# The first two half sequences of sliding-window attention: new loads, V and keys placed by products, distances added by TensorE

## The chip, the core and the metric

One core of one Trainium2 chip runs the kernel. The metric is its device time in microseconds (us), lower is better. One launch computes all four sequences and the feed-forward layer behind them.

## What is computed

The attention has four sequences of 768 tokens, 8 heads of 64. A query sees the 96 tokens up to itself and 8 global tokens at the sequence's start; the score falls with the distance, by a slope for each head. A gated layer follows (3072 tokens, 512 to 1536 to 512).

```python
scores = scale * np.matmul(q, k.transpose(0, 1, 3, 2))
rel = pos[:, None] - pos[None, :]
is_global = pos[None, :] < int(n_global)
is_local = (rel >= 0) & (rel < int(n_local))
keep = is_global | is_local
dist = np.where(is_global & ~is_local, float(n_local), np.abs(rel).astype(np.float32))
scores = scores - slopes[:, None, None] * dist[None, :, :]
scores = np.where(keep, scores, -1000000000.0)
a = np.exp(scores - np.max(scores, axis=-1, keepdims=True))
a = a / (np.sum(a, axis=-1, keepdims=True) + 1e-09)
x = np.matmul(a, v)   # then (tokens, heads * 64)
out = (np.maximum(x @ w_gate, 0.0) * (x @ w_val)) @ w_out
```

## The kernel before, in words

The work is cut into eight **halves** `s`: half `s % 2` of sequence `s // 2`, 384 queries each. In a half the heads go by **pairs** `p` (0 to 3). Queries lie on partitions as rows of three tokens (`(p n)`, n = 3), so a loaded row of q or k holds 768 bytes a head. The keys of a sequence lie in seven **key tiles** `j` of 128: the 8 global keys in rows 0 to 7, then 120 keys in order. A half meets tiles 0 to 3, or 2 to 6, each over a window of at most 72 x 3 queries (`spans`, `by`, `banks_of_half`). Of tile 3, half 0 has only 24 keys; columns 32 to 127 of `kT[..][p][:, 3]` are zeroed first, since a score product takes all 128 columns as its weights.

Every engine runs its instructions in the order in which the program writes them (`manual_schedule`). GpSimd (POOL) issues the loads that convert fp32 to bf16 (V and the weights), SyncE (SP) the others, q and k in fp32.

The first two halves of the kernel before:

- **Loads** (L110): q and k of half 0 by pairs on SP. V comes by key tile on POOL (`load_v`, L129, up to 120 rows x 8 heads of 64 numbers, 960 pieces), the global rows of V apart (L120) and spread to the other tiles by SP (L125). Weights in three groups for gate and value (L146, 512 pieces each).
- **Setup**: POOL makes the distances `dd` (L177 to L189), VectorE those of the global rows (L194 to L201). ScalarE turns them into the multiplicative masks `m_all`, eight exponentials of 432 columns (L209), and zeroes the unused halves of q (L203, L204). VectorE zeroes the unused columns of key tile 3 (L467, L470).
- **A pair**: `piece_cast` (L223) casts q and k by VectorE in half 0, by GpSimd in half 1. `piece_t` (L254) transposes them on TensorE, and VectorE copies q into two zero-padded halves (L259, L260) and k to key tiles (L238 to L244). `piece_qk` multiplies a key tile with both heads' queries at once (L306); ScalarE takes the exponential (L309), VectorE multiplies the mask (L318). `piece_av_wide` makes the sums (weights `ones`) and the values (weights V) of both heads in column halves of the array (L366), ScalarE takes lnd = ln and rcp = exp(-lnd) of the sums (L372, L374), and VectorE multiplies the values with rcp into `xT` (L377).
- The pairs of half 1 are woven with the first gate and value products of half 0's tokens (`ffn_pieces`: gate L408, relu L411, value L418, multiply L420, output L427). The first gate product of half 1's tokens needs `xT` of all four pairs of half 1; the products that follow it form a full queue on TensorE to the end.

PSUM has 8 banks: three for scores and transposes (`qk_ps`), two for `av_ps`, three for `ff_ps`. Halves 2 to 7 take another way (casts on GpSimd, transposes by DMA) that the change leaves as it is, except for where `m_all` is made.

## Time and profile before

| | |
|---|---|
| time, median of 3 runs | 258.38 us (258.17 to 259.35) |
| profiled execution, span from first to last instruction | 256.7 us (the page gives no other time of it) |
| busy TensorE | 236.1 us, 92% |
| busy ScalarE, VectorE, GpSimd | 159.0, 140.9, 93.6 us |
| granted TensorE clock | 1.000 |
| last multiply of half 0 into xT, start and duration (L377) | 24.74, 0.56 us |
| the same of half 1 | 41.64, 0.56 us |
| HBM read, mean | 135 GB/s over the span |

The profile lists each instruction's start and duration, and for idle time what ended it. Durations of TensorE products include a tail in which the next one already runs: four products of 384 columns, 326 ns each, take 0.65 us together. Several equal instructions are merged into one line with a count ("x4").

### The profile page before, as it was taken

Reading aid. Unit: us, or ns where it says so; the run is one execution under the profiler, and the core shown is the slowest. Engines: PE = TensorE matmul, PEld = TensorE weight load, DVE = VectorE, ACT = ScalarE, POOL = GpSimd, SP = SyncE. Lnnn points to the kernel's source line nnn. Section 1 sums busy time; section 2 is a strip of 40 time slices with the busy share of each in tenths; the row PEclk is TensorE's granted clock in tenths of the full one; section 3 lists DMA queues with packets and bytes.
Section 4 is the critical chain, followed back from the end, with each engine's and each line's share of the span. In section 5 each row is a group of like instructions: output and inputs, shape, how many; then the busy total and the mean of one; then the engine's idle time right before and its main releaser. Section 6 shows DMA issues by size and latency. Waiting matters only on the chain.

```text
span 256.7 us, 4693 instructions
## 1 busy us (share of the span) xinstructions
PE 236.1 (92%) x1608; PEld 138.7 (54%) x1608; DVE 140.9 (55%) x369; ACT 159.0 (62%) x321; POOL 93.6 (36%) x232
## 2 busy tenths in 40 slices
PE   1467888999999999999999999999999999999994
PEld 0235554566554566655665566556665566556541
DVE  6785895564644276625674376725763557614410
ACT  8747485333578577756875577747774677643311
POOL 8951796057635605800645145500640000000000
PEclk9999999999999999999999999999999999999999
DMA  6999699997967993856571975927451200021012
GB/s 167 204 190 234 167 195 200 231 153 153 278 83 191 189 299 70 142 79 190 171 147 11 195 250 114 116 82 223 129 125 42 82 3 0 0 82 43 0 41 83
DMA packets 82696, 34.35 MB, mean 134 GB/s; under 512 B 58609, under 2 KB 79601, under 8 KB 82673
## 3 DMA queue, kind: packets, MB, share of 16 engines
q1 hardware_dynamic: 50816, 26.16, 38.0%
q0 software_dynamic: 31856, 7.91, 31.3%
q8 instruction: 12, 0.20, 0.4%
q14 instruction: 12, 0.09, 0.1%
HBM read 28.38 MB, written 6.29 MB: 135 GB/s over the span
## 4 chain that ended last, share of the span: by engine, by line
PE 77%; DVE 11%; DMA 5%; ACT 3%; issue 1%; SPq 1%; POOL 0%; DVEq 0%; ACTq 0%; POOLq 0%
PE ff_ps L427 24%; PE ff_ps L418 22%; PE ff_ps L408 21%; PE av_ps L334 5%; PE qk_ps L306 4%; DMA ks<-in_k_dram 4%; DVE xT L351 2%; DVE es L318 2%; DVE ht L420 2%; PE qk_ps L254 1%; DVE qk L223 1%; DMA qs<-in_q_dram 1%; ACT lnd L343 1%; ACT rcp L348 1%; DVE qT L260 1%
## 5 line engine op out<-in xcount | busy, mean ns | idle before, releaser
L408 PE MATMUL ff_ps<-xT,wg 128*128 128x384 bf16 x384 | 78.4, 326 | 0.6 <-DVE ks L158 0.4
L418 PE MATMUL ff_ps<-xT,wv 128*128 128x384 bf16 x384 | 78.0, 326 | 0.6 <-DVE ht L420 0.3
L411 ACT ACTIVATE grelu<-ff_ps 128x384 bf16<-128x384 f32 x96 | 47.0, 489 | 38.3 <-DVE ht L420 21.9
L420 DVE TENSOR_TENSOR ht<-ff_ps,grelu 128x384 bf16<-128x384 f32 x96 | 53.2, 555 | 27.5 <-PE ff_ps L418 23.9
L427 PE MATMUL ff_ps<-wo_sb,ht 128*128 128x512 bf16 x288 | 67.1, 379 | 0.0
L309 ACT ACTIVATE es<-qk_ps 128x432 bf16<-128x432 f32 (+2 forms) x96 | 49.4, 529 | 17.9 <-PE qk_ps L306 15.5
L318 DVE TENSOR_TENSOR es<-es,m_all 128x432 bf16<-128x432 bf16 (+6 forms) x144 | 43.0, 335 | 22.9 <-ACT es L309 22.4
L351 DVE TENSOR_TENSOR xT<-av_ps,rcp 64x384 bf16<-64x384 f32 x48 | 26.7, 555 | 45.7 <-ACT rcp L348 41.2
L418 PEld LDWEIGHTS <-wv 128*128 128x128 bf16 x384 | 36.4, 97 | 24.2 <-issue 2.8
L408 PEld LDWEIGHTS <-wg 128*128 128x128 bf16 x384 | 36.3, 98 | 22.9
L427 PEld LDWEIGHTS <-ht 128*128 128x128 bf16 x288 | 26.9, 97 | 27.8
L306 PE MATMUL qk_ps<-qT,kT 128*128 128x432 bf16 (+6 forms) x144 | 33.7, 303 | 1.6 <-ACT es L309 1.2
L264 POOL CAST kc<-ks 128x384 bf16<-128x384 f32 x24 | 12.3, 552 | 55.8 <-DMA ks<-in_k_dram 47.9
L343 ACT ACTIVATE lnd<-av_ps 64x384 f32<-64x384 f32 x48 | 23.3, 485 | 11.1 <-PE av_ps L334 10.4
L432 ACT COPY osb<-ff_ps 128x512 f32<-128x512 f32 x24 | 14.0, 585 | 24.4 <-PE ff_ps L427 23.5
L129 POOL DMA_DIRECT2D vbuf<-in_v_dram x28 | 24.4, 879 | 0.8 <-issue 0.4
L334 PEld LDWEIGHTS <-vbuf 128*128 128x128 bf16 x216 | 18.1, 98 | 8.2 <-issue 0.7
L334 PE MATMUL av_ps<-es,vbuf 128*128 128x216 bf16 (+4 forms) x216 | 21.1, 226 | 0.5 <-DVE xT L351 0.5
L306 PEld LDWEIGHTS <-kT 128*128 128x128 bf16 x144 | 14.3, 102 | 12.2 <-issue 3.1
L272 POOL CAST qz<-qs 128x192 bf16<-128x192 f32 x48 | 14.8, 356 | 3.6 <-DMA qs<-in_q_dram 3.6
L254 PE MATMUL qk_ps<-ident,qk 128*128 128x128 bf16 x48 | 5.3, 265 | 11.6 <-DVE qk L223 9.1
L348 ACT ACTIVATE rcp<-lnd 128x384 f32<-128x384 f32 x24 | 12.5, 522 | 0.8
(68 smaller groups left out, 111.6 us busy)
## 6 DMA issues: line engine op xcount, KB each, us to landing
out_dram<-osb SPq DMA_DIRECT2D x24, 256.0 KB
ks<-in_k_dram SPq DMA_DIRECT2D x6, 768.0 KB
qs<-in_q_dram SPq DMA_DIRECT2D x6, 768.0 KB
vbuf<-in_v_dram POOLq DMA_DIRECT2D x24, 120.0 KB, 5.8
ks<-in_k_dram SPq DMA_DIRECT2D x8, 192.0 KB
qs<-in_q_dram SPq DMA_DIRECT2D x8, 192.0 KB
wg<-in_moe_w_gate_dram POOLq DMA_DIRECT2D x3, 512.0 KB, 7.4
wv<-in_moe_w_val_dram POOLq DMA_DIRECT2D x3, 512.0 KB, 9.2
```

Of the source, the lines that this page charges most:

```text
L129: nc.gpsimd.dma_start(out=v_dst(b, NG + r0, NG + r0 + n, j), in_=v[b, :, KT * j + r0 : KT * j + r0 + n, :].rearrange("h p d -> p h d"))
L306: nc.tensor.matmul(ps[:, c : c + n_], lhsT=kt[:, j, :], rhs=qd[:, :, :, a : a + w], start=True, stop=True)
L309: nc.scalar.activation(es[:, 0:cols], ps[:, 0:cols], AF.Exp, bias=0.0, scale=scale)
L318: nc.vector.tensor_mul(e4, e4, mk)
L334: nc.tensor.matmul(av3[:, :, a : a + w], lhsT=vb[:, j, z0 : z0 + 128], rhs=es[:, c : c + NN * w].rearrange("k (n p) -> k n p", n=NN), star ...
L343: nc.scalar.activation(ln[o0 : o0 + 64], av[d0 : d0 + 64, 0:QH], AF.Ln, bias=0.0, scale=1.0)
L351: nc.vector.tensor_tensor(xT_of[s][r, p, :], av_of[s, p, e_][r, 0:QH], rc[r], op=ALU.mult)
L408: nc.tensor.matmul(psg[:, 0:QH], lhsT=w_of(wg, dc, fc), rhs=xT[:, dc, :], start=(dc == 0), stop=(dc == N_DC - 1))
L411: nc.scalar.activation(gr, psg[:, 0:QH], AF.Relu, bias=0.0, scale=1.0)
L418: nc.tensor.matmul(psv[:, 0:QH], lhsT=w_of(wv, dc, fc), rhs=xT[:, dc, :], start=(dc == 0), stop=(dc == N_DC - 1))
L420: nc.vector.tensor_tensor(ht[:, fc, :], psv[:, 0:QH], st["gr"], op=ALU.mult)
L427: nc.tensor.matmul(ps2, lhsT=ht[:, fc, n * 128 : (n + 1) * 128], rhs=wo_sb[:, fc, :], start=(fc == 0), stop=(fc == N_FC - 1))
```

## The change

The first two halves get code of their own; the rest is as before.

- **q and k**: of half 0, pairs 0 and 1 come in fp32 on the SP and ACT queues and are cast; the other pairs, and all of half 1, come by casting loads on POOL (`kq0b`, `kq1`) and are used as they land, head by head in column halves of the array (`load_n`).
- **Keys of half 0**: a product with a selection matrix `sel` (1 where a row of three holds the token) both transposes and puts them on key tiles; a GpSimd copy gives tiles 4 to 6 the global keys. Half 1 has transposes and GpSimd copies.
- **V**: one load a half in rows of three tokens (`v3`, 1024 pieces of 192 numbers), put on key tiles by three selection products of 512 columns each (six for tile 3) and a copy by VectorE (`V`) or ScalarE (`A`).
- **Distances**: TensorE adds them to the scores by a product of a scaled identity (`diag`) with `dd`; there is no mask multiply and no `m_all` in these halves. `m_all` is made among the first gate and value products of half 1's tokens.
- **Scores**: the two heads of a pair are the two row halves of the array (64 rows each), into two banks; no zero-padded q. Each exponential covers both.
- **Weights**: the first group comes in two parts (`load_w_part`, gate and value, half the columns each), the other two whole, all issued on POOL among the loads of q, k and V.
- **Order and buffers**: nine products of zeros stand ahead of TensorE's queue. Half 0 has two buffers `s` of two banks for scores, two `t` for keys and V, two `av`; half 1 one `s` (two banks), one `t`, two `av`, three `ff`. The 16 loads on POOL are all issued ahead of the zeroing of `kT` tile 3 and of the second selection matrix. Tiles of later halves (`stage`, `m_all`, `kc`, `qz`) lie where those of the first two lay and wait for their last use.

The diff, cut:

```diff
+    setupp = early.enter_context(tc.tile_pool(name="setupp", bufs=1, reuse_waits="tile"))
+    cast_pool = early.enter_context(tc.tile_pool(name="cast", bufs=2, reuse_waits="tile"))
...
+    v3 = [setupp.tile([128, H, NN * D], BF16, name=f"v3_{i}") for i in range(2)]
+    kq0 = setupp.tile([128, 2, 4, NN * D], FP32, name="kq0")
+    kq0b = setupp.tile([128, 2, 4, NN * D], BF16, name="kq0b")
+    kq1 = setupp.tile([128, 2, H, NN * D], BF16, name="kq1")
...
+    nc.sync.dma_start(out=kq0[:, 0, 0:2, :], in_=rows_of(k, 0, 0, 2))
+    nc.scalar.dma_start(out=kq0[:, 1, 0:2, :], in_=rows_of(q, 0, 0, 2))
+    nc.sync.dma_start(out=kq0[:, 0, 2:4, :], in_=rows_of(k, 0, 2, 4))
+    nc.sync.dma_start(out=kq0[:, 1, 2:4, :], in_=rows_of(q, 0, 2, 4))
+    nc.scalar.preload_act_table_set("natural_log_exp_and_others")
...
+    sidx = [setupp.tile([128, 4, 128], FP32, name=f"sidx{i}") for i in range(2)]
+    sel = [setupp.tile([128, NN, 4, 128], BF16, name=f"sel{i}") for i in range(2)]
+    nc.gpsimd.iota(sidx[0][:, :, NG:128], [[KT, 4], [1, KT]], base=0, channel_multiplier=-NN,
+                   allow_small_or_imprecise_dtypes=True)
+    nc.gpsimd.iota(sidx[0][:, :, 0:NG], [[0, 4], [1, NG]], base=0, channel_multiplier=-NN,
+                   allow_small_or_imprecise_dtypes=True)
...
+    for n in range(NN):
+        nc.vector.tensor_scalar(sel[0][:, n], sidx[0], float(n), None, op0=ALU.is_equal)
...
-    nc.vector.tensor_scalar(dd[0:NG, 1], ga, BIG, float(NL), op0=ALU.mult, op1=ALU.max)
-    nc.vector.tensor_scalar(dd[0:NG, 0], gd, BIG, float(NL), op0=ALU.mult, op1=ALU.max)
...
-    zero_q(0, 0)
-    zero_q(0, 1)
+    nc.gpsimd.dma_start(out=v3[0], in_=rows_of(v, 0, 0, H))
...
+    pick(gl[0], nlc, NL, 1, 1, BIG)
+    pick(gl[1], gl[0], 0, 1, 1, float(NL))
+    pick(dd[0:NG, 0], gl[1], last, -1, 0, BIG)
+    pick(gl[2], nlc, NL - 1, 1, 0, BIG)
+    pick(dd[0:NG, 1], gl[2], last, -1, 0, BIG)
+    for i, src in enumerate((k, q)):
+        nc.gpsimd.dma_start(out=kq0b[:, i], in_=rows_of(src, 0, 4, H))
...
+    diag = setupp.tile([128, H, 128], BF16)
     for h in range(H):
-        nc.scalar.activation(m_all[:, h], dd, AF.Exp, bias=0.0, scale=-slopes[h])
+        nc.vector.tensor_scalar(diag[:, h], ident, -slopes[h] / scale, None, op0=ALU.mult)
...
+    load_w_part(0, 0, 2)
+    for h0 in (0, 4):
+        for i, src in enumerate((k, q)):
+            nc.gpsimd.dma_start(out=kq1[:, i, h0 : h0 + 4, :], in_=rows_of(src, 1, h0, h0 + 4))
+    load_w_part(0, 2, 4)
+    nc.gpsimd.dma_start(out=v3[1], in_=rows_of(v, 1, 0, H))
+    load_w_group(1)
+    load_w_group(2)
+    for p in range(HP):
+        nc.gpsimd.memset(kT[0][p][:, 3, 32:128].bitcast(mybir.dt.uint32), 0)
+        nc.gpsimd.memset(kT[0][p][:, 6, NG + 48 : 128].bitcast(mybir.dt.uint32), 0)
+    nc.gpsimd.iota(sidx[1][:, :, NG:128], [[KT, 4], [1, KT]], base=3 * KT - QH, channel_multiplier=-NN,
+                   allow_small_or_imprecise_dtypes=True)
+    nc.gpsimd.memset(sidx[1][:, :, 0:NG], -1.0)
+    for n in range(NN):
+        nc.gpsimd.tensor_scalar(sel[1][:, n], sidx[1], float(n), None, op0=ALU.is_equal)
...
+    def first_keys(p, data, of, copy_q):
+        kt = psum["t"].tile([128, 512], FP32, name="t_ps")
+        w = 3 * 128 + 32
+        for n in range(NN):
+            for lhsT, r in of(data[0], n):
+                nc.tensor.matmul(kt[r, 0:w], lhsT=lhsT,
+                                 rhs=sel[0][:, n].rearrange("t j r -> t (j r)")[:, 0:w],
+                                 start=(n == 0), stop=(n == NN - 1), skip_group_check=True)
+        tq = psum["t"].tile([128, 512], FP32, name="t_ps")[:, 0 : QH // 2].bitcast(BF16)
+        transposes(tq, data[1], of)
+        nc.vector.tensor_copy(kT[0][p].rearrange("d j r -> d (j r)")[:, 0:w], kt[:, 0:w])
+        copy_q(qTb[0][:, p, 0, :], tq)
+        nc.gpsimd.tensor_copy(kT[0][p][:, 4:NT, 0:NG],
+                              kT[0][p][:, 0:1, 0:NG].to_broadcast([128, NT - 4, NG]))
+    def second_keys(p):
...
-            for n in range(NN):
-                nc.tensor.matmul(tp[:, i, n * 128 : (n + 1) * 128],
...
-        qd = qTb[s % 2][:, p]
-        nc.vector.tensor_copy(qd[0:64, 0, :], tp[0:64, 0, :])
-        nc.vector.tensor_copy(qd[64:128, 1, :], tp[64:128, 0, :])
-        put_keys(nc.vector.tensor_copy, nc.vector.tensor_copy, kt, tp[:, 1, :], half)
+            transposes(tp[:, i], kq1[:, i, 2 * p : 2 * p + 2, :], load_n)
+        nc.vector.tensor_copy(kNb[1][:, p], tp[:, 0])
+        nc.vector.tensor_copy(qTb[1][:, p, 0, :], tp[:, 1])
+        put_keys(nc.gpsimd.tensor_copy, nc.gpsimd.tensor_copy, kT[0][p], kNb[1][:, p], 1)
+    def first_values(half, jj, copy):
+        vt = psum["t"].tile([128, 512], FP32, name="t_ps")
+        todo = [(half, n) for n in range(NN)]
+        if half == 1 and jj == 0:
+            todo += [(0, n) for n in range(NN)]
+        for i, (h_, n) in enumerate(todo):
+            nc.tensor.matmul(vt, lhsT=sel[h_][:, n, jj if h_ == half else 3, :],
+                             rhs=v3[h_][:, :, n * D : (n + 1) * D], start=(i == 0), stop=(i == len(todo) - 1))
+        j = jj + 3 * half
+        copy(v_dst(0, 0, 128, j), vt.rearrange("r (h d) -> r h d", d=D))
+        if j > 3:
...
+    def first_scores(s, p, g):
+        half = s % 2
+        spans_ = [by[half, j] for j in steps_of[half][g]]
+        ps = psum["s"].tile([128, 2, 512], FP32, name="s_ps")
+        es = es_pool.tile([128, 2, 360], BF16, name=f"ef{g}")
...
+        for e in range(2):
+            c = 0
+            for i, (j, a, w, m) in enumerate(spans_):
+                nc.tensor.matmul(ps[:, e, c : c + NN * w].rearrange("k (n t) -> k n t", n=NN),
+                                 lhsT=diag[:, 2 * p + e],
+                                 rhs=dd[:, 0 if j == 0 else 1, :, m : m + w],
+                                 start=(i == 0), stop=False, skip_group_check=True)
+                c += NN * w
+        c = 0
+        for i, (j, a, w, m) in enumerate(spans_):
+            for e in range(2):
+                r = slice(64 * e, 64 * e + 64)
+                nc.tensor.matmul(ps[:, e, c : c + NN * w].rearrange("k (n t) -> k n t", n=NN),
+                                 lhsT=kT[0][p][r, j, :], rhs=qd[r, :, a : a + w],
+                                 start=False, stop=(i == len(spans_) - 1), skip_group_check=True)
+            es_of[s, p, j] = (es, c)
+            c += NN * w
+        nc.scalar.activation(es[:, :, 0:cols], ps[:, :, 0:cols], AF.Exp, bias=0.0, scale=scale)
     def piece_cast_k(s, p):
...
+    def first_av(s, p):
+        half = s % 2
+        todo = [by[half, j] for g in steps_of[half] for j in g]
+        av = [psum["av"].tile([128, 512], FP32, name="av_ps") for _ in range(2)]
...
+                                     lhsT=ones if what == 0 else vbuf[0][:, j, z0 : z0 + D],
...
+    def first_norm(s, p):
+        av = av_of[s, p]
...
+    V, A = nc.vector.tensor_copy, nc.scalar.copy
+    stack = open_psum(s=2, t=2, av=2)
+    for _ in range(9):
+        nc.tensor.matmul(psum["av"].tile([128, 512], FP32, name="av_ps"), lhsT=zeros[:, 0:128],
+                         rhs=zeros, start=True, stop=True)
+    kq = [(kq0b[:, 0, 2 * p : 2 * p + 2], kq0b[:, 1, 2 * p : 2 * p + 2], load_n) for p in range(2)]
+    d0 = first_cast(0)
+    first_keys(0, d0, d0[2], A)
+    first_scores(0, 0, 0)
+    d1 = first_cast(1)
+    first_scores(0, 0, 1)
+    first_keys(1, d1, d1[2], V)
+    first_scores(0, 1, 0)
+    first_values(0, 0, V)
+    first_scores(0, 1, 1)
+    first_values(0, 1, A)
+    first_values(0, 2, V)
+    first_values(0, 3, A)
+    first_keys(2, kq[0], load_n, V)
+    first_av(0, 0)
+    first_scores(0, 2, 0)
+    first_scores(0, 2, 1)
+    first_keys(3, kq[1], load_n, V)
+    first_norm(0, 0)
+    first_av(0, 1)
+    first_scores(0, 3, 0)
+    first_scores(0, 3, 1)
+    first_norm(0, 1)
+    first_av(0, 2)
+    first_norm(0, 2)
+    first_av(0, 3)
+    first_norm(0, 3)
+    stack.close()
+    ff_stack = open_psum(ff=3)
+    ctx.enter_context(ff_stack)
+    stack = open_psum(t=1, s=1, av=2)
...
+    F = [f for _, f in f1_0[0 : 2 * GW]]
+    for f in (F[0], F[1], lambda: second_keys(0), F[2], lambda: second_keys(1),
+              lambda: first_scores(1, 0, 0), F[3], lambda: first_scores(1, 0, 1),
+              lambda: second_keys(2), F[4], lambda: first_scores(1, 1, 0), F[5],
+              lambda: second_keys(3), lambda: first_scores(1, 1, 1),
+              lambda: first_values(1, 0, V), lambda: first_values(1, 1, A), F[6],
+              lambda: first_values(1, 2, V), lambda: first_values(1, 3, A),
+              lambda: first_av(1, 0), lambda: first_scores(1, 2, 0), lambda: first_norm(1, 0),
+              lambda: first_scores(1, 2, 1), F[7], lambda: first_av(1, 1), lambda: first_scores(1, 3, 0),
+              lambda: first_norm(1, 1), lambda: first_scores(1, 3, 1), lambda: first_av(1, 2),
+              lambda: first_norm(1, 2), lambda: first_av(1, 3), lambda: first_norm(1, 3)):
+        f()
+    stack.close()
+    early.close()
...
+    m_all = pool.tile([128, H, 2, NN, WQ], BF16)
+    kc = [pool.tile([128, NN, DM], BF16, name=f"kc{i}") for i in range(2)]
+    qz = [pool.tile([128, NN, HP, 2, 128], BF16, name=f"qz{i}") for i in range(2)]
...
-    weave(f1_0[G[0]], spread(attention_pieces(1), 0.1, 1.6),
-          [(0.9, lambda: load_w_group(2)), (0.95, lambda: load_w(wo_sb, moe_w_out, 0, DM))])
+    load_w(wo_sb, moe_w_out, 0, DM)
...
-    weave(f1_1[G[0]])
+    weave(f1_1[G[0]], spread([(0.0, lambda h=h: nc.scalar.activation(
+        m_all[:, h], dd, AF.Exp, bias=0.0, scale=-slopes[h])) for h in range(H)], 0.0, 1.0))
```

## Prediction

> **What bounds the kernel now.** I read the page's slices first, then the chain that ended last, then the stretch up to the end of the first two halves in order of time.
>
> ```profile
> PE   1467888999999999999999999999999999999994
> ...
> POOL 8951796057635605800645145500640000000000
> ...
> PE 77%; DVE 11%; DMA 5%; ACT 3%; issue 1%; SPq 1%; POOL 0%; DVEq 0%; ACTq 0%; POOLq 0%
> ```
>
> A slice is 6.4 us. From the seventh on TensorE is full and has three quarters of the chain, so nothing there can shrink by this change. Only the first six slices, up to 42 us, can. Half 1's own loads are on that chain now:
>
> ```profile
> 17.05 9.84 DMA ks<-in_k_dram
> ```
>
> From the stretches (columns: length, then busy time of PE, PEld, DVE, ACT, POOL):
>
> ```profile
> 18.20:25.30 7.10, 5.67 (x73) 4.14 (x72) 4.42 (x15) 5.81 (x13) 0.50 (x1) 1.00 1.26 225
> 25.30:33.30 8.00, 7.13 (x57) 4.45 (x56) 6.45 (x20) 4.29 (x10) 6.29 (x15) 1.00 0.77 178
> 33.30:42.20 8.90, 7.11 (x100) 4.40 (x100) 7.90 (x31) 7.22 (x16) 8.90 (x21) 1.00 1.22 198
> ```
>
> Half 0 ends with its last xT multiply at 24.74 + 0.56 = 25.3 us, half 1 at 41.64 + 0.56 = 42.2; half 1 thus took 16.9 us with four gate and four value products inside. After 42.2 there are 256.7 - 42.2 = 214.5 us, which I carry over. The median, 258.38, lies 1.7 above the span; I add that at the end.
>
> **The step that decides: GpSimd's queue.** The order of time shows what a DMA issue costs there (start, duration, engine):
>
> ```profile
> 3.03 1.06 POOL L120 DMA_DIRECT2D vbuf<-in_v_dram  x1
> ...
> 4.09 3.61 POOL L129 DMA_DIRECT2D vbuf<-in_v_dram  x4
> ...
> 6.77 0.10 DVE L467 MEMSET kT<- 128x48 uint32 x1
> ...
> 7.69 0.80 POOL L146 DMA_DIRECT2D wg<-in_moe_w_gate_dram  x1
> ...
> 8.46 0.80 POOL L146 DMA_DIRECT2D wv<-in_moe_w_val_dram  x1
> ...
> 9.20 0.61 POOL L478 MEMSET vbuf<- 128x544 uint32 x1
> ```
>
> The issues run one behind another, a memset behind them waits its turn: 0.90 us each for 960 pieces (L129), 0.77 for the 512 of a weight group (L146). The zeroing of key tile 3's unused columns, on VectorE at 6.77 now, moves to GpSimd **behind 16 DMA issues**. I count: start 0.84; iota of 480 columns 0.6 (216 start 0.28 apart); small iota 0.15; ident 0.26; rel 0.37, sub 0.46, dd 0.55 (their spacings now): 3.2. The v3 issue, 1024 pieces, 0.93: 4.15. Five selects on 8x216 at 0.44 (the spacing of sel): 6.35. Then kq0b 2, weights 2, kq1 4, weights 2, groups 4: 14 issues of 512 pieces at 0.77 = 10.8, and v3 of half 1, 0.93: **18.1**. Bounds: all 16 at the cheapest row (0.61, a later L120) 15.3, all at 0.90 20.
>
> Who waits: the scores of (half 0, pair 0, group 1) take all 128 columns of key tile 3, so their third product waits for that memset. Behind it in TensorE's queue stands the whole rest of half 0, and ScalarE and VectorE wait for TensorE. Until then only pair 0's keys and group 0 are through (casts end near 4.4, dd complete at 6.35, exponential near 8). The nine zero products, the second load queue and the early casts buy nothing: 10 us of idle TensorE lie behind them.
>
> **Half 0 from 18.1.** Durations used: 128x384 ScalarE 0.49 and 0.52 (lnd, rcp), 128x512 0.585, 480 columns 0.568, so 720 columns 0.77; VectorE 0.36 for a bf16 PSUM copy of 384, 0.555 for a multiply of 384 fp32, so 0.58 for kT's 416 and 0.65 for V's 512; TensorE 0.65 per four products of 384 columns, 0.42 ns a column. The row-half products have no row: alone they cost 0.42 ns a column, wholly in pairs half. The nearest row is the column-half one, eight av products of 1200 columns in 0.45 us with the tail of about 0.17, so they overlap; I take that, near half.
>
> It starts cold: six transposes took 0.82 at 4.47 and 12.14 but 0.50 at 26.16, though the granted clock reads 1.00 throughout; after 10 us idle I double TensorE's first 3.5 us. Pair 1's keys and copies: q in place at 20.4. Its scores, V tile 0, scores: 22.3. V tiles 1 to 3 share two banks with their copies: last one copied at 25.15. Transposes 0.2, av 0.55, scores of pair 2 0.75: TensorE at 26.65. Now ScalarE leads: exponentials to 27.9, lnd and rcp to 28.9, multiply 29.4 (it frees the av bank), av of pair 1 29.7, pair 3's scores 30.4, its exponentials 31.7, pair 1's norm 32.7, pair 2's 33.75, multiply 34.3; av of pair 3's sums went at 33.85, its norm ends 35.0, multiply **35.6**. So 17.5 us (14 where it stays warm and overlaps, 20 where it stays cold).
>
> **Half 1.** Work on TensorE: gate and value products 5.2, transposes 1.6, distances 5568 columns 2.3, scores 1.2 to 2.3, V 15 products of 512 3.2, av 2.4: 16 to 17 us (half 0 by the same prices: keys and transposes 2.9, distances 2.0, scores 1.5, V 2.6, av 2.2, 11.2). ScalarE: exponentials 6, norms 4, relu 2, two V copies 1.2: 13. Neither sum is the time, because `s` and `t` now have one buffer each. From half 0's end, with F0 to F7 for the gate and value products of the diff's list: F0, F1, keys 0, F2, keys 1, scores, exponential: 4.3. Three more rounds of products 0.55, tail 0.2, exponential 0.75, hop 0.1: 1.6 each, 9.3 with the F between. V: keys 3's copy frees `t` at 8.75; six products and a copy, 10.95; three rounds of 0.65 + 0.2 + 0.65: 15.55. GpSimd copies the global rows of V (8x512, 0.6): 16.2; av 16.45. Then scores, exponential 17.9, norm 18.95, exponential 19.7, scores and exponential 21.4, norm 22.4, exponential 23.2, norms 24.2 and 25.2, multiply **25.8**. Bounds: 18 (TensorE's sum with a tail of 1.5), 28 (16 switches of shape at 0.09 and the tails after them 0.05 longer). I take 25.8: the buffers are written in the diff.
>
> **What is removed and added without a price.** The mask multiplies (1.15 to 1.2 us of VectorE per pair), zeroed q, key spreading, fewer V packets: VectorE isn't late in my list, so nothing. If it were, the multiplies would be worth up to 9 us (8 pairs). Half 1's loads leave the chain: kq1 is issued by 14, and even with the 9.84 us of the row above it has landed at 24, before half 1 starts at 35.6; V's second load, issued at 15, with the 5.8 us to landing of such loads at 21. Were half 1 to start at 25, they would still be hidden. m_all's eight exponentials move into half 1's gate products after 42.2: 0.49 + 2 x 0.47 per 1.3 us pair of products, 0.1 over, four times: **0.4**. wo's load, the qz clearing and V loads slide back with half 1's end; now kT is ready at 62.2 and used at 65.8, so 3.6 us cover them; a delay beyond it costs its excess, 0 to 2.
>
> **Sum.** 18.1 + 17.5 + 25.8 = 61.4 against 42.2: +19.2, with m_all +19.6; span 276.3, time 278.0.
>
> A switch between whole products and column halves: the value products of 32.59 are all issued at 33.24 and the av products start at 33.33, so 0.09 at most; no row shows row halves. Sixteen scores with two switches each make 2.9 by it, half of them in half 1, which the upper bound holds. A rule speaks against the change here: the Trainium skill, TensorEngine Tiling (Array Packing), Key Properties, says that changing the tiling mode drains TensorE. If each switch waited out a whole tail (0.326 of a product less its 0.16 spacing), the 32 would add 5.3 by this rule, and the sum would be 281 where the row leaves it at 278. The second rule is of the clock: TensorE: Matmul & The Clock Gate, Part 1, has the full clock come after some 3.4 us of activity and go again after an idle window as long. The cold and warm rows above agree with the first part; no run here shows the second, and if idleness took nothing away half 0 would be some 1.7 shorter by it.
>
> **Rivals.** (1) The wait is there, but half 1 overlaps down to TensorE's sum, 18: 35.6 + 18 = 53.6, time 270. For: 28 to 32 us now is full; against: one score buffer. (2) The memset isn't late (the issues cost little when rows are 768 bytes): V lands at 4.15 + 5.8 = 10, pair 1's second exponential ends at 11.65 and not at 23.1, so half 0 ends 11.4 earlier, at 24.2, half 1 at 50.0: 266.6. Against: L146's rows are larger still and cost 0.77. (3) **Faster**: the same, and both halves run at TensorE's sum: 6.4 + 11.2 + 16.5 + tails 3 = 37.1, time 253.7. It decides below T0 = 8 and a half 1 under 18 together; each has evidence against it. (4) Also the following loads come late and TensorE stays cold: 285 to 288.
>
> **How the numbers follow.** The three stretches with all bounds at one end make 47.3 and 68, times 264 and 286; they hardly fall to one side together, so the forecast's own range is 272 to 284: 0.70. Rival 1 0.13, rival 2 0.08, rival 3 0.04, rival 4 0.05. The time is the forecast's, a little toward rival 1's side: 277. The range runs from 268, which takes most of rival 1, to 284. Faster by over 0.5%, which is about what a measurement here can tell: 0.04 (rival 3); within it 0.02; slower 0.94.
>
> **What would show it.** A wait of TensorE of about 10 us, near 8 us, ended by GpSimd's memset of kT; 16 issues in a row on POOL before it; the last xT multiply of half 0 near 35.6 and of half 1 near 61; in half 1 TensorE waiting on the exponentials and on the V copies; the remaining 214.5 us unchanged. The prediction is wrong if the memset starts before 10 us, or half 1 takes under 19 us.

## The result, and the profile after

The changed kernel takes 285.08 us (median of four executions, 283.22 to 286.24) against 258.87 for the kernel before on the same chip: **slower, ratio 1.0997, 95% interval 1.0937 to 1.1057**. The profiled execution took 285.34, with a span of 283.6 us and a mean granted clock of 0.958. The prediction was 277, range 268 to 284: the direction and the wait that it names hold, the size is too small by 8, and the time lies just outside the range.

The page of the changed kernel: busy tenths of TensorE and GpSimd in 40 slices of 7.1 us, the granted clock of TensorE in the same slices, and the chain that ended last.

```profile
PE   7109789777999999999999999999999999999994
...
POOL 8967003268356526056206360670063000000000
PEclk9857959979999999999999999999999999999999
...
PE 79%; DMA 7%; DVE 5%; POOL 4%; ACT 3%; issue 1%; POOLq 0%; DVEq 0%; ACTq 0%
```

The first three slices of TensorE, 7, 1 and 0, are the zero products with pair 0's first work and then nothing. GpSimd is busy just there (8967). GpSimd, which the chain of before hardly touched, now has 4% of it. From the eleventh slice on TensorE's row is as full as before. The clock row has a dip that begins in the empty slices and reaches into the fourth, and two more, in the sixth and the ninth, where TensorE works.

What TensorE waited for (total, times, longest, us):

```profile
PE s_ps L356 <- POOL kT L248: 13.0, 1, 13.0
PE av_ps L464 <- ACT lnd L474: 2.7, 4, 1.2
PE s_ps L347 <- ACT ef L361: 1.6, 2, 0.8
PE t_ps L330 <- DVE vbuf L333: 1.6, 2, 0.8
```

One wait of 13.0 us, of a score product for GpSimd's zeroing of kT, is half of the loss. The others shown are short waits on exponentials, norms and V copies; none is over 1.2 (only the first zero product, at the start, waits 1.3).

The order of time around that wait (start, duration, engine; in brackets the idle time before and what ended it):

```profile
15.26 0.89 POOL L244 DMA_DIRECT2D v<-in_v_dram  x1 [1.21 <-DMA wg<-in_moe_w_gate_dram]
16.59 0.75 POOL L150 DMA_DIRECT2D wg<-in_moe_w_gate_dram  x1 [0.44 <-DMA wv<-in_moe_w_val_dram]
17.75 0.74 POOL L150 DMA_DIRECT2D wv<-in_moe_w_val_dram  x1 [0.40 <-DMA kq<-in_k_dram]
18.79 0.74 POOL L150 DMA_DIRECT2D wg<-in_moe_w_gate_dram  x1 [0.30 <-DMA kq<-in_q_dram]
19.87 0.74 POOL L150 DMA_DIRECT2D wv<-in_moe_w_val_dram  x1 [0.34 <-DMA kq<-in_k_dram]
20.60 0.16 POOL L248 MEMSET kT<- 128x48 uint32 x1
...
20.81 0.20 PE L356 MATMUL s_ps<-qT,kT 64*128 64x24 bf16 x2 [12.96 <-POOL kT L248]
```

The issues cost what was foreseen, 0.74 to 0.89 us. New are the brackets: from its twelfth load on GpSimd itself waits, each time for the landing of an earlier load, 1.21 + 0.44 + 0.40 + 0.30 + 0.34 = 2.7 us in all. By the names in the brackets the twelfth load waits for the fourth, the thirteenth for the fifth, and so on, always the load eight before.

The stretches (length, then busy us of PE, PEld, DVE, ACT, POOL, then granted clock, DMA share, GB/s):

```profile
11.82:20.60 8.78, 0.00 (x0) 0.00 (x0) 0.00 (x0) 0.00 (x0) 6.08 (x10) 0.50 1.42 171
20.60:25.48 4.88, 4.64 (x25) 2.41 (x27) 1.31 (x3) 1.34 (x2) 4.79 (x14) 0.50 1.45 199
25.48:35.72 10.24, 8.10 (x101) 4.67 (x98) 3.20 (x7) 5.43 (x10) 1.53 (x5) 1.00 1.05 174
35.72:42.54 6.82, 5.94 (x52) 3.88 (x51) 2.17 (x4) 3.10 (x7) 0.00 (x0) 0.50 0.00 0
42.54:59.61 17.07, 13.69 (x151) 7.67 (x147) 4.96 (x13) 6.75 (x11) 7.28 (x26) 1.00 0.02 2
59.61:63.02 3.41, 3.41 (x33) 1.83 (x32) 1.12 (x2) 1.29 (x2) 1.85 (x7) 0.50 1.10 161
...
68.66:283.60 214.94, 209.87 (x1345) 122.05 (x1344) 107.36 (x256) 132.22 (x268) 64.51 (x167) 1.00 0.62 119
```

Half 0 ends at 40.04 (its last multiply into xT, 39.48 + 0.56), half 1 at 68.66 (68.10 + 0.56). The last column but two is what the prediction lacked: TensorE ran at half clock not only in the wait and behind it (11.8 to 25.5) but again from 35.7 to 42.5 and from 59.6 to 63.0. The rest, 214.94 us, agrees with the 214.5 of before and 0.4 for m_all.

The kernel before did not run at full clock throughout, as the 1.000 of its page suggests. Its records of the clock begin at 21.3 us only, and the page counts the time ahead of them as full. But six transposes take 0.82 us there at 16.10 and 0.50 at 26.16, and 128x432 score products follow one another every 360 ns (0.83 ns a column), against 0.42 ns a column later: TensorE ran at half clock up to 21.3 us. In the changed kernel the records begin at 5.0 us, and its zero products ahead of that run at 0.83 ns a column too.

So the first two halves cost 68.66 - 42.2 = 26.5 us, which is the whole difference. Three questions stay: is the one memset the cause of half of it; is the clock the cause of what is over; and is the remainder the price of the parts or of their order?

### The profile page after: what moved, and what is told of

It is laid out like the page before. It is cut to its first block, busy times and chain, and to the rows that moved or that the text cites. A ratio compares the mean times of both kernels' runs of the same rounds, so it can differ in the third digit from the quotient of the medians.

```text
span 283.6 us, 4950 instructions
## 1 busy us (share of the span) xinstructions
PE 255.5 (90%) x1788; PEld 147.6 (52%) x1788; DVE 127.4 (45%) x306; ACT 157.4 (56%) x311; POOL 100.6 (35%) x250
## 4 chain that ended last, share of the span: by engine, by line
PE 79%; DMA 7%; DVE 5%; POOL 4%; ACT 3%; issue 1%; POOLq 0%; DVEq 0%; ACTq 0%
PE ff_ps L520 22%; PE ff_ps L501 21%; PE ff_ps L511 20%; PE av_ps L434 5%; DMA wo_sb<-in_moe_w_out_dram 4%; PE qk_ps L406 4%; DMA kq<-in_k_dram 3%; PE t_ps L330 3%; DVE xT L451 2%; DVE ht L513 1%; ACT ef L361 1%; PE av_ps L464 1%; PE s_ps L347 1%; PE t_ps L287 1%; PE s_ps L356 1%
## 5 line engine op out<-in xcount | busy, mean ns | idle before, releaser
L511 PE MATMUL ff_ps<-xT,wv 128*128 128x384 bf16 x384 | 79.4, 330 | 0.6 <-DVE ht L513 0.3
L513 DVE TENSOR_TENSOR ht<-ff_ps,grelu 128x384 bf16<-128x384 f32 x96 | 53.3, 555 | 31.8 <-PE ff_ps L511 24.8
L409 ACT ACTIVATE es<-qk_ps 128x432 bf16<-128x432 f32 (+2 forms) x72 | 37.8, 528 | 10.7 <-PE qk_ps L406 8.9
L418 DVE TENSOR_TENSOR es<-es,m_all 128x432 bf16<-128x432 bf16 (+5 forms) x108 | 32.4, 329 | 23.0 <-ACT es L409 22.5
L364 POOL CAST kc<-ks 128x384 bf16<-128x384 f32 x24 | 11.7, 530 | 53.2 <-DMA ks<-in_k_dram 49.5
L361 ACT ACTIVATE ef<-s_ps 128x720 bf16<-128x720 f32 (+2 forms) x16 | 11.1, 708 | 27.9 <-PE s_ps L356 27.8
L406 PE MATMUL qk_ps<-qT,kT 128*128 128x432 bf16 (+5 forms) x108 | 24.7, 286 | 0.0
L434 PEld LDWEIGHTS <-vbuf 128*128 128x128 bf16 x216 | 18.1, 98 | 8.2 <-issue 0.7
L133 POOL DMA_DIRECT2D vbuf<-in_v_dram x21 | 18.2, 875 | 0.2 <-issue 0.2
L278 POOL COPY kT<-kN 128x240 bf16<-128x240 bf16 x16 | 6.8, 425 | 29.9 <-DVE kN L320 15.0
L356 PE MATMUL s_ps<-qT,kT 64*128 64x216 bf16 (+6 forms) x72 | 5.6, 240 | 13.0 <-POOL kT L248 13.0
```

What stands on the lines that cost most here:

```text
L133: nc.gpsimd.dma_start(out=v_dst(b, NG + r0, NG + r0 + n, j), in_=v[b, :, KT * j + r0 : KT * j + r0 + n, :].rearrange("h p d -> p h d"))
L406: nc.tensor.matmul(ps[:, c : c + n_], lhsT=kt[:, j, :], rhs=qd[:, :, :, a : a + w], start=True, stop=True)
L409: nc.scalar.activation(es[:, 0:cols], ps[:, 0:cols], AF.Exp, bias=0.0, scale=scale)
L418: nc.vector.tensor_mul(e4, e4, mk)
L434: nc.tensor.matmul(av3[:, :, a : a + w], lhsT=vb[:, j, z0 : z0 + 128], rhs=es[:, c : c + NN * w].rearrange("k (n p) -> k n p", n=NN), star ...
L511: nc.tensor.matmul(psv[:, 0:QH], lhsT=w_of(wv, dc, fc), rhs=xT[:, dc, :], start=(dc == 0), stop=(dc == N_DC - 1))
```

## The experiments

All times are medians of two executions (zeroing behind 9 loads, two `t` with zeroing on VectorE, no distance products, V by key tiles) to twelve. "Half 0 ends" and "half 1 ends" are the ends of the last multiply into xT of each, and with the span come from the profiled execution. In the last three kernels the two halves overlap. The kernels ran on several chips, on which the kernel before takes 258.6 to 259.4; the ratio is to the kernel before on the same chip, so two kernels are better compared by their ratios than by differences of 1 us.

| kernel | time | ratio to before, interval | half 0 ends | half 1 ends | span |
|---|---|---|---|---|---|
| before | 258.4 to 259.4 | | 25.30 | 42.20 | 256.7 |
| changed | 285.08 | 1.0997 (1.0937 to 1.1057) | 40.04 | 68.66 | 283.6 |
| zeroing on VectorE | 268.13 | 1.0375 (1.0322 to 1.0428) | 24.81 | 53.45 | 268.3 |
| zeroing behind 9 loads | 274.03 | 1.0586 (1.0521 to 1.0651) | 31.64 | 57.69 | 272.6 |
| 12 loads, not 16 | 281.12 | 1.0814 (1.0764 to 1.0865) | 36.14 | 64.68 | 279.4 |
| TensorE kept busy | 282.04 | 1.0875 (1.0816 to 1.0933) | 37.16 | 63.22 | 278.0 |
| two `t` in half 1 | 280.11 | 1.0818 (1.0768 to 1.0868) | 39.76 | 64.90 | 279.6 |
| two `t`, zeroing on VectorE | 266.01 | 1.0252 (1.0186 to 1.0318) | 24.86 | 49.68 | 264.4 |
| no distance products | 267.66 | 1.0316 (1.0227 to 1.0404) | 24.20 | 49.63 | 267.2 |
| V by key tiles | 265.47 | 1.0231 (1.0164 to 1.0298) | 28.10 | 48.84 | 263.9 |
| all parts, new order | 261.95 | 1.0102 (1.0067 to 1.0136) | 26.64 | 38.51 | 260.3 |
| the same, loads earlier | 257.73 | 0.9951 (0.9926 to 0.9975) | 26.56 | 38.43 | 256.1 |
| the same, half 1's V by key tiles | 257.48 | 0.9964 (0.9928 to 1.0000) | 25.70 | 36.91 | 254.8 |

### Where the zeroing stands in GpSimd's queue

Theory: TensorE's queue waits for GpSimd's memset of key tile 3, which stands behind 16 load issues. Rival: something else of half 0 is late anyway, and the wait only moves. The first kernel gives the memset to VectorE, the second leaves it on GpSimd but ahead of the last seven loads.

```diff
+    d0 = first_cast(0)
+    for p in range(HP):
+        nc.vector.memset(kT[0][p][:, 3, 32:128].bitcast(mybir.dt.uint32), 0)
...
-        nc.gpsimd.memset(kT[0][p][:, 3, 32:128].bitcast(mybir.dt.uint32), 0)
```

> The zeroing of key tile 3's columns goes from behind GpSimd's 16 loads to VectorE, behind the first cast. Queue theory (TensorE's whole queue waits for that zeroing): the wait of 13.0 us goes, half 0 ends at 24 to 27 us and not at 40.0, half 1 keeps its 26 to 28.6, the time is 267 to 271. Rival (another thing behind the same loads is as late, V's load, the casting loads of pairs 2 and 3, or GpSimd's own copies): a new wait of over 5 us takes its place, half 0 ends after 31, the time stays over 275.

> The zeroing stays on GpSimd but stands ahead of the second part of the first weights, so behind 9 loads: it runs at about 12.5 us and not at 20.6. Queue theory: half 0 ends 8.1 us earlier, near 31.9, the time is about 277. Rival (the products behind are bound by something else): less than 4 us of it are seen.

With the memset on VectorE the 13.0 us wait is gone and none takes its place: the longest wait of TensorE in the whole execution is 1.3 us, at the start. Half 0 ends at 24.81 and the time falls by 17 us, to 268.13. On GpSimd behind nine loads, where nothing waits for a landing yet, the memset runs at 12.55, TensorE waits 4.9 us, and half 0 ends at 31.64, as expected. The time, 274.03, is 3 us under the expected 277: from 18.3 us on this execution kept the full clock, and half 1 took 26.05 instead of 28.62. So the place of one line of the program, four memsets of 0.16 us, is worth 17 of the 26 us, the slow clock behind the wait included. What is left, 9 us, is half 1: it ends 11.3 us later than before the change in the profiled execution, the slowest of its four (270.06).

### Whether GpSimd waits for the load eight before

The same bytes in twelve loads: the first weight group whole, q and k of half 1 in one load each.

```diff
-    load_w_part(0, 0, 2)
-    for h0 in (0, 4):
-        for i, src in enumerate((k, q)):
-            nc.gpsimd.dma_start(out=kq1[:, i, h0 : h0 + 4, :], in_=rows_of(src, 1, h0, h0 + 4))
-    load_w_part(0, 2, 4)
+    load_w_group(0)
+    for i, src in enumerate((k, q)):
+        nc.gpsimd.dma_start(out=kq1[:, i], in_=rows_of(src, 1, 0, H))
```

> The changed kernel with the same bytes in 12 GpSimd loads ahead of the zeroing rather than 16: first weight group in two whole loads, q and k of half 1 in one load each. In the changed kernel GpSimd's 12th to 16th loads waited 1.21, 0.44, 0.40, 0.30 and 0.34 us, each for the landing of the load eight before it. If the number of loads decides: nothing waits up to the 11th load, the 12th at most 1.5 us, the zeroing runs at 15.5 to 17 us instead of 20.6, the time is 279 to 281. Rival (bytes or pieces under way decide, whose total is the same): the waits come to 2 us or more again, the zeroing at 17.5 to 19, time 281.5 to 284.

GpSimd in order of time, in this kernel:

```profile
16.02 0.74 POOL L150 DMA_DIRECT2D wv<-in_moe_w_val_dram  x1 [1.52 <-DMA wg<-in_moe_w_gate_dram]
16.75 0.16 POOL L246 MEMSET kT<- 128x48 uint32 x1
```

Eleven loads go out without a wait; the twelfth waits 1.52 us for the fourth. So here the number of loads decides and not the bytes: this kernel's first eleven carry more bytes than the changed kernel's. The zeroing runs at 16.75 instead of 20.60, TensorE's wait is 9.1 instead of 13.0, and the time falls by 4.0 for the 3.85 us gained.

### Whether the clock makes the rest

Theory: TensorE is slow behind the wait, and later, because its clock was lowered. Test: 57 more products of zeros fill the wait, so that TensorE never idles there.

```diff
+    for _ in range(57):
+        nc.tensor.matmul(psum["av"].tile([128, 512], FP32, name="av_ps"), lhsT=zeros[:, 0:128],
+                         rhs=zeros, start=True, stop=True)
```

> 57 products of zeros (512 columns each, some 12.3 us at full clock) stand in TensorE's queue ahead of the scores that wait; the zeroing runs at 20.6 as before. Clock theory: TensorE's first 3.4 us behind the wait run at full clock, 1.5 to 2 us are saved in half 0, the time is about 283; the cold stretches near 36 to 42 and near 60 us stay. Rival (the idle time costs nothing beyond itself): the same time within 0.5 us, the three selection products behind the wait still take 1.2 us.

The stretches of half 0 from the zeroing on and of half 1 in this kernel:

```profile
20.05:37.16 17.11, 13.09 (x161) 7.93 (x160) 6.18 (x12) 9.38 (x17) 6.33 (x18) 1.00 1.08 166
37.16:63.22 26.06, 20.74 (x255) 12.15 (x255) 8.15 (x20) 12.65 (x22) 12.85 (x36) 1.00 0.35 55
```

The zeroing runs at 20.05 here. At full clock half 0 takes 17.11 us from there, against 19.44, and half 1 26.06, against 28.62, with the same instructions. That is 4.9 us of cold TensorE in the profiled executions. Product by product, the changed kernel falls behind this one by 1.56 us up to 25.5, by 1.87 between 35.7 and 42.5 (0.77 of it in half 0) and by 1.46 between 59.6 and 63.0, and by nothing in between.

All four executions of this kernel ran at a mean clock of 0.994 or more, all four of the changed one at 0.952 to 0.961. The medians differ by 3.0 only. The profiled execution, 279.77, is the fastest of its four; another, also at 1.000, took 282.20, and what its 2.4 us are isn't known. Two ran at 0.994, which one stretch of 3.4 us at half clock in 280 would make. So the later dips, expected to stay since TensorE's work there is the same, went in the profiled execution and at least mostly in the others.

What the dips follow can be read from the clock records of all thirteen kernels. Every stretch between two changes of the clock is a multiple of 3.41 us long (changed kernel: 13.65, 10.24, 6.83, 17.07 and 3.41). The step ahead of the changed kernel's first dip, 8.41 to 11.82, lies in the wait and is empty. The steps ahead of the other two:

```profile
32.31:35.72 3.41, 1.67 (x24) 1.13 (x25) 0.56 (x1) 1.60 (x4) 0.00 (x0) 1.00 0.65 106
56.20:59.61 3.41, 1.80 (x36) 1.32 (x32) 0.00 (x0) 1.59 (x3) 2.87 (x12) 1.00 0.08 7
```

TensorE was busy for 49% and 53% of them. Over the thirteen kernels, every loss of the full clock follows a step of 57% or less and none a step of 59% or more; between 42% and 57% it went both ways, without a loss after two steps of 54% in the kernel kept busy. Every return after a dip, 17 of them, follows a step of 99% or more, none a step of 85% or less. So a dip needs no idle stretch, only a step with too little work in it, and where the steps' edges fall on the same work can decide. These are readings of the records; no run varies the busy share alone.

### What half 1 is bound by

Theory: half 1 is paced by its single buffers, not by TensorE's sum. The kernel with two `t` takes one bank from `ff` for it.

```diff
-    ff_stack = open_psum(ff=3)
-    ctx.enter_context(ff_stack)
-    stack = open_psum(t=1, s=1, av=2)
+    stack = open_psum(ff=2, t=2, s=1, av=2)
+    ctx.enter_context(open_psum(ff=3))
```

> In half 1 the feed-forward products have two banks and `t` has two; all else as in the change. Buffer theory (the keys and V of half 1 wait for one bank to be copied out): the V part from 49.9 to 57.4 us shortens by 2 to 3.5 us, the time is 281 to 283. Rival (half 1 is bound by the one score buffer and the exponentials): under 1 us.

> The zeroing early, as in e1_zero_early, and two banks for keys and V in half 1, as in e4_two_t. If the two are separate waits, their gains add: 268.1 less 3.5 to 4.9 us, 263 to 265. If the single bank only showed because TensorE came late and cold, under 1 us of it is left: 267 to 268.

> e1_zero_early without the products that add the distances (left out: distance and mask; the exponentials take the bare scores). My list has 0.4 us of them in each of the 16 score groups, in half 0 behind a second score buffer, in half 1 on the path of the one buffer: half 0 within 1 us, half 1 shorter by 2.5 to 3.5 us, the time 264 to 266. Rival (TensorE's sum of work bounds both halves): 4 us or more less, split between the halves.

> e1_zero_early with V loaded by key tiles as in the kernel before (28 fewer-row loads replaced: 8 loads on GpSimd and the spreads on SP for this sequence), no selection products and no copies of V. If the V part is a third of half 1 (50.6 to 57.4 us in the changed kernel), half 1 shortens by 5 to 7 us, the time is 260 to 264, half 0 changes by less than 2 us since the pairs 2 and 3 then come later behind V's issues. Rival (V's products fill time in which half 1 waits for exponentials anyway): under 2 us.

Two `t` shorten half 1 from 28.62 to 25.14 (24.8 with the zeroing on VectorE), though TensorE does the same work. Its dip at the half's end, which cost 1.46, is gone too, so of the 3.5 us some 2.0 are left for the buffer (an estimate). With the zeroing early the second `t` takes 2.1 us off the time, or 3.2 by the ratios. The time, 266.01, lies between the two expectations.

The next two take work from TensorE, in the kernel with the early zeroing. Without the distance products, which leaves distance and mask out of the scores of these halves, half 0 ends at 24.20 instead of 24.81 and half 1 takes 25.4 instead of 28.64, at the same mean clock (0.90 and 0.89): 3.8 us less in the halves. The time falls by 0.5 only (1.5 by the ratios), outside the expected 264 to 266, and its two executions lie 2.7 apart. That kernel's rest grew to 217.6, mostly since from 49.6 to 70 us its clock was 0.90 while TensorE was full. So what these products are worth in time isn't told by this pair.

With V loaded by key tiles as before, and the selection products and copies of V gone, half 1 takes 20.7 us (18.0 of them TensorE's work), 5.3 below the 26.06 of the full clock with them, although its clock was still half in its first 2.2 us. But half 0 ends 3.3 later, at 28.10, where less than 2 was expected: the five V issues stand on GpSimd ahead of the distances of the global rows, TensorE waits 3.5 us for these, and its mean clock from 5 us to the end of half 0 was 0.75. So the time falls by 2.7 only (3.7 by the ratios), to 265.47, not to 260 to 264. V by selection is a dear part of half 1; what its fewer issues gain in half 0 isn't separated from the clock.

### All the parts in another order

If order is the cause, the parts as they are, listed otherwise, should give most of the loss back. In this kernel VectorE does the zeroing and the second selection matrix; GpSimd issues ten loads early, those of q, k and V first and the first weight group last; half 1's keys, V and first scores stand on TensorE's queue between half 0's norms (with four buffers for the exponentials); the other weights follow half 1's last key copies.

```diff
+    first_scores(0, 2, 0)
+    second_keys(1)
+    first_scores(0, 2, 1)
+    first_av(0, 1)
+    second_keys(2)
     first_norm(0, 1)
+    first_scores(1, 1, 0)
+    first_scores(1, 1, 1)
+    second_keys(0)
+    first_values(1, 2, V)
     first_av(0, 2)
...
-    load_w_group(1)
-    load_w_group(2)
...
+    load_w_group(1)
+    load_w_group(2)
```

> All parts of the change kept, the order changed: zeroing early, GpSimd's loads are 10 and q, k, V of half 1 and the first weight group come first, the second selection matrix is made by VectorE, and the keys, V tiles and half of the scores of half 1 stand among the norms of half 0, with two score and two key buffers. My list by the measured durations ends half 1 with its gate and value products at 38 us against 42.2: time 253 to 256, if the loads land as in e1_zero_early and TensorE keeps its clock; 258 to 260 if the loads of half 1 come 4 us later than I take. Rival (the new parts cost more work than the old ones and can't be hidden): over 262.

Half 1 ends at 38.51, 3.7 us earlier than before the change, with all parts in place. Yet the time is 261.95, slower by 1.0%, well over the expected 253 to 256 and just short of the rival's 262. The gain is lost further on. Of this kernel, in three views: TensorE's longest wait; the transposes on SP's queue in order of time; and what the DMA engines moved in each slice of 6.5 us.

```profile
PE qk_ps L401 <- DMA qT<-qz: 4.2, 1, 4.2
```

```profile
55.14 10.32 SPq L374 DMA_TRANSPOSE qT<-qz  x3
```

```profile
GB/s 130 156 187 117 6 183 232 223 197 179 271 139 141 165 256 166 145 89 92 237 113 69 137 299 80 141 79 193 155 144 40 81 3 0 3 81 40 1 43 81
```

Half 2's query transposes take 10.32 us (3.93 before) while the output weights, issued at 43.4, are landing, so its scores come 4.2 us late. And in the fifth slice, 26 to 32 us, the DMA engines stand nearly still (6 GB/s): the loads of the second and third weight group wait on GpSimd behind key copies that wait in turn for half 1, and the output weights stand behind these and half 2's V loads. The next kernel only moves these five issues ahead of the copies.

```diff
     first_values(1, 0, A)
+    load_w_group(1)
+    load_w_group(2)
+    load_w(wo_sb, moe_w_out, 0, DM)
     stack.close()
```

> The order of e8 with one more move: the loads of weight groups 1 and 2 and of the output weights are issued by GpSimd ahead of half 1's last key copies (about 26 us) instead of behind them and behind the memsets, in a stretch (26 to 32 us) in which e8's DMA engines moved 6 GB/s. In e8 TensorE was full to 60 us and lost 4.2 us at one wait for qT (half 2's transposes from 55.1 to 65.5, beside the landing of the output weights), and more at 65 to 70. Theory (the change itself is about worth its 3.7 us at the end of the halves, and the missing gain was taken back by late loads): halves end by 39, half 2's query transposes take about 4 us as before, span 253 to 257, time 254.5 to 258.5 (256.3 likely, 0.99 of before). Rival 1 (half 2's chain is bound by its own late q and k loads, issued at 40 us): the wait stays at 3 us or more, time 260 to 262. Rival 2 (the earlier loads collide with half 1's key copies and the loads of half 1): halves end at 41 or later, time 258 to 261.

Of this kernel the page's busy times, the same transposes and the same wait:

```profile
PE 247.4 (97%) x1788; PEld 144.0 (56%) x1788; DVE 126.3 (49%) x311; ACT 158.3 (62%) x313; POOL 93.7 (37%) x241
```

```profile
58.69 4.00 SPq L374 DMA_TRANSPOSE qT<-qz  x3
```

```profile
PE qk_ps L401 <- issue: 1.6, 1, 1.6
```

The transposes are back at 4.00, the wait is 1.6 us instead of 4.2, and the time is **257.73, ratio 0.9951 (0.9926 to 0.9975): faster than the kernel before by half a per cent**, within the expectation's 254.5 to 258.5. Since five issues moved together, the run doesn't tell which of them had slowed the transposes. Half 1 ends 3.8 us earlier than before the change, of which 1.3 us remain in the medians and 0.6 in the profiled spans: the work that follows half 1 takes 217.7 instead of 214.5. The 1.6 us that TensorE misses between 60 and 70 are that wait for half 2's first score, and there the expectation's first rival was right in part. Half 2's load of k is issued at 40.08, only 2.2 us earlier than before the change, and its first score starts at 64.73 instead of 65.81, 1.1 earlier.

TensorE is now busy 97% of the span, with 247.4 us against 236.1 before the change. The last run takes work off it: half 1's V comes by key tiles, half 0's V stays with selection products.

```diff
-    nc.gpsimd.dma_start(out=v3[1], in_=rows_of(v, 1, 0, H))
+    nc.gpsimd.memset(vbuf[0][:, NT - 1, :].bitcast(mybir.dt.uint32), 0)
+    load_v(0, 3, r0=24)
+    for j in range(4, NT):
+        load_v(0, j)
...
-    first_values(1, 2, V)
...
+                kr = slice(0, 32 if half == 0 and j == 3 else 128)
...
+                                     lhsT=ones[kr] if what == 0 else vbuf[0][kr, j, z0 : z0 + D],
```

> The order of e9, with half 1's V loaded by key tiles (four GpSimd loads in place of one) instead of selection products; half 0's V stays with selection products, and of key tile 3 they fill the 32 rows that half 0 uses, which are also all that its value products read there. It takes 15 selection products (of 27 that took 6.9 us in e9, so 3.8 us of TensorE) and four copies by VectorE and ScalarE off the first halves and adds some 2.7 us of GpSimd. Theory (in e9 TensorE's own sum is the bound: 247.4 us busy of a span of 256.1, against 236.1 of 256.7 before the change): the halves end at 34.5 to 36.5 instead of 38.5, half 2's loads start as much earlier, time 253.5 to 256. Rival 1 (with less TensorE work the halves are bound by ScalarE and the norms): halves end at 37 to 38.5, time 256.5 to 258. Rival 2 (half 1's V, loaded in pieces ahead of the first weights, lands too late or holds up half 0's value products): a wait of over 2 us at a value product, time over 258.

TensorE's busy time falls by 1.8 us, not 3.8, the halves end at 36.91 instead of 38.43, and the profiled span is 254.8 against 256.1. That lies between theory and first rival; the wait for half 2's first score is 2.0 us here. The medians, 257.48 and 257.73, don't tell the two kernels apart.

## Why the prediction was too low

**The wait held, three terms were too small.** A wait of TensorE near 8 us, ended by GpSimd's memset behind 16 issues in a row; half 1 longer than TensorE's sum; the rest unchanged: all three are in the profile. Three terms of the sum were mis-sized, all in the same direction: the queue of issues was summed without waits for landings, and both halves without the losses of the clock that came later.

| term | predicted | measured | over |
|---|---|---|---|
| zeroing on GpSimd starts | 18.1 (15.3 to 20) | 20.60 | 2.5 |
| half 0 from there | 17.5 (14 to 20) | 19.44 | 1.9 |
| half 1 | 25.8 (18 to 28) | 28.62 | 2.8 |
| the rest with m_all | 214.9 | 214.94 | 0.0 |

- **The zeroing.** "14 issues of 512 pieces at 0.77" were priced right to a few hundredths each; the first V load cost 1.10 for 0.93, the second 0.89. Without the waits the sum would be 17.9, for 18.1. What failed is the step that takes a queue of issues as the sum of its issues. From the twelfth on each waits for a landing, 2.7 us together; with twelve loads only one waits, 1.52. The bounds took the cheapest and dearest issue row, and neither holds a wait.
- **Half 0.** The prediction doubled TensorE's first 3.5 us behind the wait, at a cost of 1.7. The half clock lasted longer there, from 20.6 to 25.5, and cost 1.56. So this was right in kind and in size. What it lacked is the second dip, from 35.7 on, in which half 0's last norms stretch: 0.77. At full clock the half takes 17.11, and the list of steps, 15.8 without the clock, was 1.3 short.
- **Half 1.** 25.8 was worked out at full clock, and at full clock it takes 26.06 (26.05 in the run with the zeroing behind nine loads). The excess, 2.6, is the two dips at its start and near its end. The upper bound of 28 had room for switches of shape but none for the clock. The waits that the prediction named are there, 1.6 us on exponentials and 1.6 on V copies in the kernel kept busy; all waits together are 5.3 us, and TensorE is busy 20.7 of the 26.06, tails included. That the list came within 0.3 is partly luck, since it had no price for the switches: 16 at the scores of half 1, some 1.5 us by the price below.
- **Row halves and switches.** Taken as overlapping from the column-half row. Four score products of 192 and 168 columns, two in each row half, take 0.33 us with their tail in the reordered kernel; one behind the other they would take 0.30 without it (0.42 ns a column). So they do overlap; the records have the two of a pair start 3 ns apart. A switch has a price, though. In the kernel kept busy, the last distance product of a group, 48 columns or 20 ns of work, starts at 43.50 and the first score product at 43.62 (below). Over the work of the product before, each change from whole products to row or column halves or back mostly costs 0.09 to 0.10 us, in this kernel as in the kernel before the change. So the prediction's 0.09 was right and the 0.166 of a whole tail too much; the sum would be 283 by that tail (278 and 5.3), not 281. Half 0 has 13 switches behind the zeroing that involve row halves, which would be 1.2 of the 1.3 us missing in its list, if all were on its path; no run shows that.

```profile
43.50 0.18 PE L347 MATMUL s_ps<-dd,diag 128*128 128x48 bf16 x1
43.62 0.32 PE L356 MATMUL s_ps<-qT,kT 64*128 64x216 bf16 x6
```

- **The second cited rule.** It was that the full clock comes after some 3.4 us of activity and goes after an idle window as long. The first part agrees with one addition: work came back at 20.8 and the full clock at 25.5, at the end of the first step of 3.41 us that TensorE filled. For the second part the Trainium skill, TensorE: Matmul & The Clock Gate, Part 1, counts windows of 3.4 us, and the dips here are 13.65, 6.83 and 3.41 long, which fits them. The loss at 11.82 followed an empty window too. But those at 35.72 and 59.61 didn't: TensorE was busy 49% and 53% of the windows ahead of them, and its longest single wait there was 1.2 us.

**The rivals.** Rival 4, TensorE cold and the following loads late, had 285 to 288 and a chance of 0.05, and the measured 285.08 lies in it. Its first half is what happened; its second isn't, since the rest took 214.94. Rival 1, half 1 down to 18, fails by the 26.06 at full clock. Rival 2, a memset that isn't late, was priced at 266.6; the kernel made for it, with the zeroing on VectorE, took 268.13, with half 0's end at 24.81 for the predicted 24.2. Rival 3, both halves at TensorE's sum, gave 37.1 and 253.7; its conditions fail in the change as it is, while in another order the halves come near its 37.1 (38.4) and the time doesn't (257.7), since what follows them comes hardly earlier. "VectorE isn't late in my list" held, and so did the cover of half 1's loads: none of them shows among TensorE's waits.

**What the change is worth.** The parts trade idle TensorE for work on it: 11.3 us more busy time (236.1 to 247.4) against 20.6 us of idle before and 8.7 after, with all parts in place and the weights issued earlier. The added work is larger than that at equal clock, since in the kernel before some 10 us of the busy time, up to 21.3 us, ran at half clock. Of the 26 us of the change itself, 17 come from one memset's place in a queue; that is shown. The remaining 9 went with the new order and the earlier weights. A second `t` alone takes 2 to 3 of them; how the rest divides among buffers, cold stretches and order isn't separated, since the reordered kernel changes many things at once.

## What to carry to other kernels

Price a queue of loads as issues plus landings: look for the load whose completion each later issue must await, and put nothing that another engine needs behind it. When work moves from an idle engine onto the one that bounds the end, add both sums first; what the change can win is the idle time less the added work. And when a stage ends earlier, ask at once whether the loads of the next stage were issued earlier too.

## What the runs showed that was not expected

- By these rows GpSimd has no more than eight loads under way in this program: each later one waits for the one eight before it (1.21, 0.44, 0.40, 0.30, 0.34 us; 1.52 in the kernel with twelve).
- TensorE's clock changes in steps of 3.41 us. It fell to half after steps in which TensorE was 49% and 53% busy, without an idle stretch of that length, and came back only after a step that was full. Where between 42% and 57% the line runs stays open.
- A change between whole products and halves of the array costs 0.09 to 0.10 us of TensorE.
- The comparison that makes a third of a selection matrix, 128x512, takes a mean of 1.49 us on GpSimd (changed kernel) and on VectorE 0.56 (changed kernel) or 0.42 (reordered kernel), for the same shape and types.
